# Attention scores on the tensor engine: one product of 32 rows by 128 columns, or four of 32 rows by 32 columns

## The chip, the cores and the metric

The kernel runs on one core of one Trainium2 chip. The metric is the time of one execution on the device in microseconds (us); smaller is better. The kernel before takes 1616.93 us (median of two runs, 1616.18 and 1617.67). The profile was taken in one more execution, whose span from the first to the last instruction is 1615.1 us.

The core has a tensor engine (PE; its weight loads are listed apart as PEld), a vector engine (DVE), a scalar engine (ACT), a general engine (POOL) and queues that start transfers (SP).

## The reference

Two layers, each an attention with 32 heads of 16 elements that share one key and one value head, followed by a mixer and an MLP. Only the attention is touched. Cut to what matters (sequence 2048, width 512):

```python
def _A_ref(x, wq, wk, wv, wo):
    B, S, D = x.shape
    H = 32
    Dh = D // H                                   # 16
    q = (x @ wq).reshape(B, S, H, Dh) ...         # transposed to B, H, S, Dh
    k = x @ wk                                    # S x 16, one for all heads
    v = x @ wv
    scores = jnp.einsum("bhqd,bkd->bhqk", q, k) * (Dh ** -0.5)
    p = _softmax(scores, axis=-1)
    o = jnp.einsum("bhqk,bkd->bhqd", p, v)
    return ... o ... @ wo

x = A_x
x = x + _A_ref(_layernorm(x), A_wq, A_wk, A_wv, A_wo)
x = x + _B_ref(_layernorm(x), ...)                # mixer and MLP
x = x + _A_ref(_layernorm(x), A_wq, A_wk, A_wv, A_wo)
x = x + _B_ref(_layernorm(x), ...)
```

A score product has only 16 elements to sum over. The kernel pads them to 32, so four heads fit side by side into the 128 rows of the tensor engine.

## The kernel before

The program declares operations with their inputs, outputs and an assumed duration. A planner in the same file puts them in order when the program is built, and each engine then runs a fixed list in a fixed order with semaphore waits. Nothing is reordered at run time except what the hardware itself does.

The keys lie four times over in `KT` (rows 0-31, 32-63, 64-95, 96-127), the queries of four heads lie in the same four row groups of `QT`. One call of `qk` makes the scores of one head `h` for 128 keys (or twice 128 keys, where a chunk has only 256 queries) in one bank of `PB`, which is PSUM:

```python
def qk(self, e, g, h, bank):
    la, c, b, kb, nk = g[0:5]
    n = self.size(la, c)                 # 512 queries, or 256 (then nk = 2)
    for j in range(nk):
        ins = e.matmul(self.PB[:, bank, j * n:(j + 1) * n],
                       lhsT=self.KT[32 * h:32 * h + 32, la, (kb + j) * 128:(kb + j + 1) * 128],
                       rhs=self.QT[32 * h:32 * h + 32, self.par(la, c), b, 0:n],
                       start=True, stop=True, tile_position=(32 * h, 0))
    return ins
```

Scores leave PSUM in one of two ways. A *unit* is two heads, made together in one of two pairs of banks and turned into exponentials by one instruction of ACT. A *pair* is two heads whose exponentials are made from integer arithmetic by DVE and POOL; each head of it takes a bank of a small pool.

```python
def declare_unit(self, g):
    b0 = self.ACT_SLOTS[k % 2]                         # banks 0,1 or 2,3
    hs = (2 * g[5], 2 * g[5] + 1)
    def fpe(e):
        for j, h in enumerate(hs):
            ins = self.qk(e, g, h, b0 + j)
        return ins
    q = op("PE", fpe, ..., pe=("Q", 512, 256, hs), prio=0)
    o = q.feeds = op("ACT", lambda e: e.activation(self.EA[:, ea, :, :], self.PB[:, b0:b0 + 2, :],
                                                   ACTF.Exp, scale=0.25), ...)
    ...
def declare_pair(self, g):
    for i in range(2):
        op("PE", lambda e, h=h, L=L: self.qk(e, g, h, L.bank), ..., pe=("Q", 512, 128, (h,)))
        o = op("DVE", lambda e, ...: e.tensor_scalar(out=J[...], in0=self.PB[:, L.bank, :], ...))
    ... # two more scaled copies JK, on POOL or DVE
```

The exponentials go back into the tensor engine against the values (`VP`, `VD`), four products at a time, each with 128 rows and 32 columns, into four partition ranges of the bank `ACC`. All products of the projections, the mixer and the MLP are cut in the same way, by `dot`. Products of zeros by ones (`NIL`, `ONES`), called fillers, are put where the plan would otherwise leave the tensor engine idle, because its clock depends on how busy it is.

```python
def dot(self, e, bank, n, lhsT, rhs, start, stop):
    for g in range(4):
        ins = e.matmul(self.PB[32 * g:32 * g + 32, bank, 0:n], lhsT=lhsT[:, 32 * g:32 * g + 32], rhs=rhs,
                       start=start, stop=stop, tile_position=(0, 32 * g), skip_group_check=True)
    return ins

def declare_pv(self, seg, g, ap, tags, part):
    def fpe(e):
        for j in range(nk):
            for x in range(4):
                i, u = divmod(x, 2)
                ins = e.matmul(self.PB[32 * x:32 * x + 32, self.ACC, p * hw:p * hw + hw], lhsT=v[:, la, kb + j, :],
                               rhs=ap[:, i, j * w + u * hw:j * w + u * hw + hw], start=first and j == 0,
                               stop=False, skip_group_check=True, tile_position=(0, 32 * x))
        return ins
```

The planner knows two kinds of packed products, `"Q"` (the scores) and `"P"` (everything cut in four columns), and reckons 0.097 us for each change between them:

```python
SWITCH = 0.097
def begin(self, o, t):
    if o.pe[0] != self.pe_kind:
        return max(t, self.pe_end + self.SWITCH)
    ...
```

Of the kernel before, what the change touches and what calls it, by code (L numbers as in the profile page):

```python
# [495 lines left out]
class Kernel:  # L496
# [448 lines left out]
    def qk(self, e, g, h, bank):  # L945
        la, c, b, kb, nk = g[0:5]
        n = self.size(la, c)
        ins = None
        for j in range(nk):
            ins = e.matmul(self.PB[:, bank, j * n:(j + 1) * n],  # L950
                           lhsT=self.KT[32 * h:32 * h + 32, la, (kb + j) * 128:(kb + j + 1) * 128],
                           rhs=self.QT[32 * h:32 * h + 32, self.par(la, c), b, 0:n],
                           start=True, stop=True, tile_position=(32 * h, 0))
        return ins

    def filler(self):
# [518 lines left out]
```

The softmax here doesn't subtract the row's maximum and nothing guards it: scores larger than these inputs give would overflow.

## Time and profile before

The profile has 28,953 products and as many weight loads on PE.

| engine | busy us | share of the span | instructions |
|---|---|---|---|
| PE | 1567.6 | 97% | 28953 |
| PEld | 654.9 | 41% | 28953 |
| ACT | 1500.5 | 93% | 1580 |
| DVE | 1245.5 | 77% | 2222 |
| POOL | 1118.4 | 69% | 1083 |

Busy time is the union of the recorded intervals. The recorded interval of a product is longer than the time for which it keeps the next one waiting, because products are pipelined and their ends are modelled; so 97% on PE does not say that PE has no pauses. The starts of the products are the sounder record. The granted clock of PE is 0.999 of full speed over the span. Transfers play no part: 13 GB/s on average.

In the tables of groups, a row gives the source line, the engine, the operation, what is written and read, the tile of the array (rows*columns), the moving operand's shape, the count, then busy time and the mean duration of one, then the idle time of the engine before it and what ended it.

### The profile page before, as it was taken

The page shows a single profiled execution, that of the slowest core. Times are in us where ns is not written, and L with a number is a line of the kernel's source. Part 1 is how long each engine was busy: PE and PEld are TensorE (multiplying, and loading weights), DVE is VectorE, ACT ScalarE, POOL GpSimd, SP SyncE. Part 2 cuts the span into 40 slices and gives each one's busy share as a digit, 9 for nine tenths or more (in the row PEclk, how much of TensorE's full clock was granted, in tenths as well). Part 3 has the DMA queues.
Part 4 walks back from the last instruction along what each step waited for, and adds up shares of the span by engine and source line. Part 5 has one row for each costly group of instructions (what it writes and reads, how often), then busy time and mean ns, then how long its engine had stood idle before and what let it go on. Part 6 is the DMA issues. An engine that isn't in the chain of part 4 may idle for free.

```text
span 1615.1 us, 63788 instructions
## 1 busy us (share of the span) xinstructions
PE 1567.6 (97%) x28953; PEld 654.9 (41%) x28953; DVE 1245.5 (77%) x2222; ACT 1500.5 (93%) x1580; POOL 1118.4 (69%) x1083
## 2 busy tenths in 40 slices
PE   8999999999999999999999999999999999999999
PEld 3333333434333333333333434333343334544555
DVE  8777887778887679887776678878678885778863
ACT  4999999999999999999998499999999998999952
POOL 4798877866787766776673477677777867768631
PEclk9999999999999999999999999999999999999999
DMA  6100010001000001000000000100000000000000
GB/s 207 17 6 5 7 18 6 6 4 17 7 6 4 6 4 19 6 4 2 2 2 2 3 9 9 19 4 5 9 18 5 6 5 15 16 8 7 6 17 19
DMA packets 32144, 21.55 MB, mean 13 GB/s; under 512 B 12672, under 2 KB 31360, under 8 KB 31872
## 3 DMA queue, kind: packets, MB, share of 16 engines
q1 hardware_dynamic: 31872, 17.47, 4.5%
q8 instruction: 226, 3.70, 1.0%
q14 instruction: 46, 0.38, 0.1%
HBM read 7.90 MB, written 2.10 MB: 6 GB/s over the span
## 4 chain that ended last, share of the span: by engine, by line
ACT 64%; PE 33%; DVE 2%; issue 0%; DMA 0%; POOL 0%; SPq 0%; POOLq 0%
ACT EA L994 59%; PE PB L612 12%; PE PB L950 10%; PE PB L1073 8%; ACT G L1403 2%; PE PB L769 1%; ACT L994 1%; ACT GP L1323 1%; ACT L1403 1%; ACT L1323 0%; DVE ZR L752 0%; DVE ST L723 0%; DMA X<-in_A_x_dram 0%; DVE J L1015 0%; PE PB L878 0%
## 5 line engine op out<-in xcount | busy, mean ns | idle before, releaser
L994 ACT ACTIVATE EA<-PB 128x1024 bf16<-128x1024 f32 x1504 | 1390.6, 1105 | 66.6 <-PE PB L1073 33.8
L1025 POOL TENSOR_SCALAR JK<-J 128x1024 uint16<-128x1024 uint16 x983 | 1035.6, 1054 | 402.4 <-DVE J L1015 257.4
L1015 DVE TENSOR_SCALAR J<-PB 128x512 uint16<-128x512 f32 x1088 | 702.4, 683 | 185.1 <-PE PB L950 181.1
L950 PE MATMUL PB<-QT,KT 32*128 32x512 bf16 (+1 forms) x4608 | 624.4, 359 | 30.5 <-ACT EA L994 18.6
L1073 PE MATMUL PB<-EA,VP 128*32 128x256 bf16 (+1 forms) x6784 | 388.4, 265 | 0.5
L950 PEld LDWEIGHTS PB<-QT,KT 32*128 32x128 bf16 x4608 | 161.3, 91 | 448.0 <-ACT EA L994 351.4
L1073 PE MATMUL PB<-JK,VD 128*32 128x256 bf16 (+1 forms) x4864 | 291.3, 265 | 2.9 <-POOL JK L1025 1.9
L1073 PEld LDWEIGHTS PB<-EA,VP 128*32 128x32 bf16 x6784 | 157.1, 95 | 175.3 <-issue 149.6
L612 PE MATMUL PB<-ONES,NIL 128*32 128x512 bf16 x1984 | 177.1, 387 | 7.4 <-DVE ZR L752 2.8
L1073 PEld LDWEIGHTS PB<-JK,VD 128*32 128x32 bf16 x4864 | 114.9, 95 | 128.0 <-issue 78.8
L612 PE MATMUL PB<-ZT,W 128*32 128x512 bf16 (+2 forms) x2816 | 166.6, 341 | 0.0
L1073 PE MATMUL PB<-J,VD 128*32 128x256 bf16 (+1 forms) x2432 | 154.9, 264 | 1.3 <-DVE J L1015 0.8
L612 PE MATMUL PB<-W,G 128*32 128x512 bf16 x1792 | 122.9, 380 | 0.3 <-DVE X L1279 0.3
L1396 DVE CAST G<-PB 128x512 bf16<-128x512 f32 (+2 forms) x126 | 72.3, 582 | 34.7 <-PE PB L612 33.4
L612 PEld LDWEIGHTS PB<-ZT,W 128*32 128x32 bf16 x2816 | 67.7, 96 | 26.1 <-issue 13.0
L1025 DVE TENSOR_SCALAR JK<-J 128x1024 uint16<-128x1024 uint16 x105 | 73.2, 702 | 2.9 <-PE PB L1073 1.9
L1073 PEld LDWEIGHTS PB<-J,VD 128*32 128x32 bf16 x2432 | 60.6, 95 | 35.4 <-issue 21.6
L612 PEld LDWEIGHTS PB<-ONES,NIL 128*32 128x32 bf16 x1984 | 49.6, 96 | 42.4 <-issue 11.2
L745 POOL TENSOR_TENSOR SM<-SM,MH 128x4 f32<-128x4 f32 (+4 forms) x30 | 31.7, 1058 | 40.8 <-DVE SM L737 24.8
L1133 DVE TENSOR_TENSOR OS<-ACCF,PB 128x512 bf16<-128x512 bf16 (+1 forms) x72 | 44.6, 622 | 17.7 <-PE PB L1127 17.3
L612 PEld LDWEIGHTS PB<-W,G 128*32 128x32 bf16 x1792 | 42.2, 96 | 31.8 <-issue 11.7
L1403 ACT ACTIVATE G<-G 128x3584 bf16<-128x3584 bf16 (+2 forms) x18 | 46.0, 2601 | 9.4 <-DVE G L1396 9.3
(88 smaller groups left out, 861.5 us busy)
## 6 DMA issues: line engine op xcount, KB each, us to landing
OT<-OS SPq DMA_DIRECT2D x424, 8.0 KB, 1.8
W<-in_B_w_dram SPq DMA_DIRECT2D x2, 1792.0 KB, 14.4
QT<-QS SPq DMA_DIRECT2D x40, 64.0 KB, 2.4
X<-in_A_x_dram SPq DMA_DIRECT2D x8, 256.0 KB, 5.4
out_dram<-OUTB SPq DMA_DIRECT2D x16, 128.0 KB, 1.7
OT<-OS SPq DMA_DIRECT2D x104, 4.0 KB, 1.7
W<-in_B_w_dram SPq DMA_DIRECT2D x2, 512.0 KB, 8.4
WQ<-in_A_wq_dram SPq DMA_DIRECT2D x1, 512.0 KB, 5.0
```

The source lines that it names most:

```text
L612: ins = e.matmul(self.PB[32 * g:32 * g + 32, bank, 0:n], lhsT=lhsT[:, 32 * g:32 * g + 32], rhs=rhs, start=start, stop=stop, tile_position= ...
L745: op("POOL", lambda e: e.tensor_tensor(out=self.SM[:, 0:k, a:b], in0=self.SM[:, 2:2 + k, a:b], in1=self.MH[:, 0:k, a:b], op=ALU.pow), read ...
L769: ins = e.transpose(self.PBH[:, L.bank, j * 512 + i * 128:j * 512 + (i + 1) * 128], self.ZR[:, tb % 4, dc * 128:(dc + 1) * 128], self.IDENT)
L950: ins = e.matmul(self.PB[:, bank, j * n:(j + 1) * n], lhsT=self.KT[32 * h:32 * h + 32, la, (kb + j) * 128:(kb + j + 1) * 128], rhs=self.QT ...
L994: o = q.feeds = op("ACT", lambda e: e.activation(self.EA[:, ea, :, :], self.PB[:, b0:b0 + 2, :], ACTF.Exp, scale=0.25), writes=bk + [("EA" ...
L1015: o = op("DVE", lambda e, i=i, L=L: e.tensor_scalar(out=J[:, i * 512:(i + 1) * 512], in0=self.PB[:, L.bank, :], scalar1=128 * LOG2E * 0.25 ...
L1025: x = op(eng, lambda e, k=k, r=r: e.tensor_scalar(out=self.JK[:, r, :], in0=J, scalar1=float(self.STEPS[k]), scalar2=1.0, op0=ALU.add, op1 ...
L1073: ins = e.matmul(self.PB[32 * x:32 * x + 32, self.ACC, p * hw:p * hw + hw], lhsT=v[:, la, kb + j, :], rhs=ap[:, i, j * w + u * hw:j * w + ...
L1133: op("DVE", lambda e: e.tensor_tensor(out=self.OS[:, m, 0:n], in0=acc, in1=self.PB[:, M.bank, 0:n], op=ALU.mult), reads=[("ACCF", m)], wri ...
L1323: return e.activation(self.GP[:, par, :, 2:2 + n], self.GP[:, par, :, 2:2 + n], ACTF.Gelu_apprx_tanh)
L1396: op("DVE", lambda e, f=f, L=L: e.tensor_copy(self.G2[:, f, 0:n], self.PB[:, L.bank, 0:n]), writes=[L, ("G2", f)], dur=t_ps(n), give=L)
L1403: ins = e.activation(self.G2[:, a:a + 7, 0:n], self.G2[:, a:a + 7, 0:n], ACTF.Gelu_apprx_tanh)
```

## The change

Each score product with a stationary operand of 32 rows by 128 columns becomes four products with 32 rows by 32 columns. The four take consecutive quarters of the same 128 keys as stationary operand, read the same queries as moving operand, and write the four partition ranges of the same bank. The results and their places are unchanged. The form of the score products comes nearer to that of all the others, whose columns are already cut in four. The order of the operations is not touched, because the costs that the planner assumes are not touched.

```diff
@@ -947,10 +947,12 @@
         n = self.size(la, c)
         ins = None
         for j in range(nk):
-            ins = e.matmul(self.PB[:, bank, j * n:(j + 1) * n],
-                           lhsT=self.KT[32 * h:32 * h + 32, la, (kb + j) * 128:(kb + j + 1) * 128],
-                           rhs=self.QT[32 * h:32 * h + 32, self.par(la, c), b, 0:n],
-                           start=True, stop=True, tile_position=(32 * h, 0))
+            for x in range(4):
+                k0 = (kb + j) * 128 + 32 * x
+                ins = e.matmul(self.PB[32 * x:32 * x + 32, bank, j * n:(j + 1) * n],
+                               lhsT=self.KT[32 * h:32 * h + 32, la, k0:k0 + 32],
+                               rhs=self.QT[32 * h:32 * h + 32, self.par(la, c), b, 0:n],
+                               start=True, stop=True, tile_position=(32 * h, 32 * x), skip_group_check=True)
         return ins
```

## The prediction

> **What bounds the kernel now.** I read the chain of work that ended last first, then the groups, then single products on PE. The chain and the rows of the groups that matter:
>
> ```profile
> ACT 64%; PE 33%; DVE 2%; issue 0%; DMA 0%; POOL 0%; SPq 0%; POOLq 0%
> ACT EA L994 59%; PE PB L612 12%; PE PB L950 10%; PE PB L1073 8%; ACT G L1403 2%; PE PB L769 1%; ACT L994 1%; ACT GP L1323 1%; ACT L1403 1%; ACT L1323 0%; DVE ZR L752 0%; DVE ST L723 0%; DMA X<-in_A_x_dram 0%; DVE J L1015 0%; PE PB L878 0%
> ...
> L994 ACT ACTIVATE EA<-PB 128x1024 bf16<-128x1024 f32 x1504 | 1390.6, 1105 | 66.6 <-PE PB L1073 33.8
> ...
> L950 PE MATMUL PB<-QT,KT 32*128 32x512 bf16 (+1 forms) x4608 | 624.4, 359 | 30.5 <-ACT EA L994 18.6
> ```
>
> The exponentials of ACT (L994) carry 59% of the chain, and PE 33%, of which the score products (L950), the only line that changes, 10%. ACT waits for PE in all only 66.6 us before its exponentials. The table of stretches shows where: ACT is full in most of the attention, and not full where the projections of a chunk come on top (columns: length, then PE, PEld, DVE, ACT, POOL busy with counts, clock of PE, share and rate of transfers).
>
> ```profile
> 300.00:400.00 100.00, 98.67 (x1746) 40.36 (x1744) 75.43 (x132) 99.69 (x104) 69.77 (x67) 1.00 0.03 6
> ...
> 800.00:900.00 100.00, 96.06 (x1666) 40.93 (x1658) 72.44 (x135) 81.82 (x83) 54.29 (x53) 1.00 0.01 2
> 900.00:1000.00 100.00, 96.87 (x1724) 39.58 (x1720) 72.22 (x131) 87.37 (x93) 66.54 (x64) 1.00 0.04 8
> ...
> 1300.00:1400.00 100.00, 97.97 (x2134) 43.46 (x2136) 70.19 (x122) 92.68 (x95) 67.16 (x65) 1.00 0.05 13
> ```
>
> How full PE really is has to be read from the starts of its products. The timeline of PE (start, length, then the group):
>
> ```profile
> 429.87 0.39 PE L950 MATMUL PB<-QT,KT 32*128 32x512 bf16 x2
> 430.19 0.29 PE L1073 MATMUL PB<-EA,VP 128*32 128x256 bf16 x4
> 430.31 0.28 PE L1073 MATMUL PB<-JK,VD 128*32 128x256 bf16 x4
> 430.52 0.65 PE L950 MATMUL PB<-QT,KT 32*128 32x512 bf16 x4
> 431.10 0.29 PE L1073 MATMUL PB<-EA,VP 128*32 128x256 bf16 x4
> 431.22 0.60 PE L612 MATMUL PB<-ONES,NIL 128*32 128x512 bf16 x8
> 431.76 0.39 PE L950 MATMUL PB<-QT,KT 32*128 32x512 bf16 x2
> ```
>
> Two score products start together at 429.87 and the next kind starts 0.32 us later: 512 columns at 2.4 per ns are 0.213, so 0.1 is the change of kind. From 430.31 to 430.52 it is 0.21 for 256 columns (0.107): 0.1 again on the way back. The four products of one value group (x4) start 3.4 ns apart in the single records. I went through all starts: after subtracting the streams (1218 us, with the 3.4 ns steps inside the groups), and 3226 changes of kind at 0.098 us (316 us), only 95 us of pauses are left on PE in the whole span, 56 of them before score products. (The three sums exceed the span by 14 us, because inside one kind the steps of a group hide behind the stream of the group before; ahead of a change of kind they don't.) So PE is nearly as full as ACT. Another sign: a unit's score products may start 56 ns after the exponential that frees their banks (5th percentile), but the median starts after 228 ns, and between 300 and 400 us after 353 ns. Exponentials end 917 ns apart (median), and PE is close behind them.
>
> **What the Trainium skill says.** "TensorEngine Tiling (Array Packing)", section Key Properties, says that a change of tiling mode drains the engine, while different tiles of one mode run in parallel. The trace agrees: 94 to 101 ns at each change, whatever the two shapes (32*128 to 128*32 101, 128*128 to 128*32 96, 32*128 to 128*128 103), and about nothing inside a kind. "TensorE: Matmul & The Clock Gate", section Measured speedup vs the span model, gives about 4 ns per further tile in a pack, up to sixteen tiles of 32 by 32. The trace shows 3.4 ns for four column tiles, and for up to four row tiles too: the time from the first score product of a run to the next kind is 314, 318, 321 and 325 ns for runs of 1, 2, 3 and 4 products of 512 columns (medians of 6, 815, 129 and 365 runs). No run here has sixteen. The same page, section Weight-path perf modes, says that a fast weight load needs all 128 columns, so the change gives it up. In the trace this looks harmless: recorded loads are 91 ns for 128 columns and 92 to 96 for 32, and the first group after a change of kind is longer by 10 to 11 ns in both forms (278 against 267 ns for scores of 256 columns, 283 against 272 for values).
>
> **The change part by part.** It removes 4608 products and loads and puts 18,432 in their place, 13,824 more of each. The streams do not grow: the four quarters run side by side. Waits, semaphores, banks and order stay. What is added is the step inside the group: 13,824 x 3.43 ns (the mean of 20,378 such steps) = 47.4 us of PE. Checked by runs: there are 1528 runs of score products between other kinds, so 31 ns each: 6 more steps (21 ns) in 815 runs of two, 12 more (42 ns) in 365 of four. I expect the change of kind to cost the same: the row size still changes from 32 to 128, and a change of the rows alone (32*128 to 128*128) cost 103 ns. So nothing is gained there.
>
> How much of the 47 us reaches the end? By the chain: L950 holds 9.9% of the span (160 us); at about 0.32 us per run that is 500 runs, times 31 ns = 15.5 us. By stretches: the added time per 100 us is the count of score products x 3 x 3.43 ns, for 300 to 400 us 274 x 10.3 = 2.8 us, against 2.7 us of pauses left on PE there. From 100 us on the pauses per 100 us are 10.7, 6.0, 2.7, 5.9, 3.5, 4.8, 3.5, 7.1, 8.1, 5.8, 4.4, 6.1, 3.6, 4.3; the added time is 2.0 to 3.3, with 3.8 at 1300 and 5.6 at 1400, where a run has twice as many products. If half of the pauses can take it up, and none of those between 800 and 1000, where PE is already on the chain, about 16 us are left over; if a third can, about 24. I take 20: 1617 + 20 = 1637.
>
> **The rivals.** First, the change is free: ACT sets the pace, PE catches up in its pauses, and the time stays within a few us of 1617. For it: ACT waits only 0.7 us for PE between 100 and 700 us. Against it: the late starts (353 ns of some 420 that a unit can be late before ACT idles: 917 less 56 less the 384 to 388 of the products less a second 56). Second, the change of kind gets cheaper, since both kinds now have 32 columns. That would be worth 0.1 us at most of 3226 changes, and ACT would then cap the gain: its 66.6 us of waiting and the 33% of PE in the chain allow perhaps 50 us, to 1570. Against it: 32*128 to 128*128 drains as long as any other change. Third, the loads of 32 columns in one row group don't overlap, and each further quarter costs some tens of ns in place of 3.4; at 25 ns it would be 13,824 x 25 = 346 us, past 1900. Against it: the value groups load four column tiles of the same rows 3.4 ns apart. Fourth, PE's sequencer becomes the bound: between 1400 and 1500 us it would have to issue 2695 + 3 x 548 = 4339 products, one per 23 ns. For it: no stretch shows that rate for long; the fastest 128 products in a row took 2.90 us (22.6 ns each), the fastest 256 took 27.8 ns each. Against it: "TensorEngine Tiling", section Instruction Overhead, gives some 60 cycles per product, but 32 products of 128 columns start here 13.9 ns apart, and no change of kind in the dense part is late without a semaphore (88 to 89 ns in 117 cases). It would add 10 to 30 us in the last 250 us, to about 1660. The clock is a last doubt: if quarter tiles counted less as activity it would fall; the tile area in use is the same, so I give it little.
>
> **Range and chances.** The sum is 0 to 47 us if the step of 3.4 ns holds. Ends of 1619 (nearly all hidden) and 1662 (all exposed, or part of it and some of the fourth rival) should hold it 8 times in 10. Slower by over 2% means above 1649, 32 of the 47 us exposed, or rival three or four: 0.28. Faster by over 2% needs the second rival: 0.03. Within 2%: 0.69.
>
> **What would show it.** Right: 42,777 products on PE; steps of 3.4 ns inside score groups of 8; 338 ns from the first score product of a unit to the next kind, and 366 ns for four heads; about 0.1 us at each change; pauses before score products down from 56 us to some 30; late starts of units up; idle time of ACT before L994 up from 66.6 to 80 to 90 us, most of it where PE is on the chain; clock at 1.00. Wrong: steps well above 3.4 ns or loads that end the wait (third rival), changes of kind under 80 ns (second), stretches at 1370 to 1550 us that lose far more than 5 us per 100 us (fourth), or a clock below 0.95.

## The result, and the profile after

The changed kernel takes 1692.44 us (median of two runs, 1689.84 and 1695.05) against 1616.93: 75.5 us more, a ratio of 1.0465 with a 95% interval of 1.0445 to 1.0485. The prediction was 1637 with a range of 1619 to 1662.

The page of the kernel after first: the clock by slices, the chain that ended last by engine and by line, and the rows of the exponentials (now L996) and of the score products (now L952).

```profile
PEclk9999999999999999999999999999999998997999
...
PE 53%; ACT 41%; DVE 3%; issue 2%; POOL 1%; DMA 0%; SPq 0%; POOLq 0%
ACT EA L996 38%; PE PB L952 19%; PE PB L612 16%; PE PB L1075 15%; PE PB L769 2%; ACT G L1405 1%; DVE J L1017 1%; ACT L996 1%; PE PB L1129 1%; ACT GP L1325 0%; ACT L1405 0%; POOL JK L1027 0%; PE PB L1114 0%; DVE ZR L752 0%; PE PB L811 0%
...
L996 ACT ACTIVATE EA<-PB 128x1024 bf16<-128x1024 f32 x1504 | 1416.7, 1062 | 113.4 <-PE PB L952 73.0
...
L952 PE MATMUL PB<-QT,KT 32*32 32x512 bf16 (+1 forms) x18432 | 677.3, 364 | 34.0 <-ACT EA L996 13.9
```

PE has taken over the chain (53% for 33%), ACT waits 113.4 us before exponentials (66.6 before), and late in the run there are slices in which the clock was granted only in part. Before, there were none.

Where the time went shows when the same exponential is looked up in both traces: there are 1504, in the same order, counted from 0 here. The table gives how much later each one ends in the changed kernel (worked out from the single records):

| exponential | ends, before | later by |
|---|---|---|
| 250th | 254.7 us | 0.9 us |
| 500th | 502.3 us | 5.4 us |
| 800th | 804.9 us | 10.4 us |
| 1300th | 1337.6 us | 19.2 us |
| 1350th | 1399.3 us | 28.8 us |
| 1400th | 1450.2 us | 40.3 us |
| 1450th | 1496.2 us | 56.0 us |
| 1503rd | 1549.3 us | 72.9 us |

Up to the 1300th the loss is a slow drift, 19 us in 1300. In the last 200 exponentials it is 54 us. These belong to the last two chunks of the second layer, which have 256 queries in place of 512, so that every product of the attention has half the columns and there are twice as many. Two stretches of 20 us from there (columns: length, then PE, PEld, DVE, ACT and POOL busy with counts, clock, share and rate of transfers), before and then after:

```profile
1440.00:1460.00 20.00, 19.77 (x526) 9.38 (x518) 15.79 (x29) 19.94 (x20) 14.81 (x16) 1.00 0.03 7
```

```profile
1440.00:1460.00 20.00, 17.64 (x700) 8.75 (x697) 12.82 (x25) 17.39 (x19) 10.31 (x10) 1.00 0.05 9
```

The changed kernel has 700 products in 20 us, 28.6 ns each, while PE is *less* busy than before (17.64 for 19.77) and so is every other engine. Its timeline on PE shows what the missing time looks like (start, length, group, then idle time and what ended it):

```profile
1434.92 0.29 PE L1075 MATMUL PB<-JK,VD 128*32 128x128 bf16 x8
1435.04 0.28 PE L1075 MATMUL PB<-EA,VP 128*32 128x128 bf16 x8
1435.15 0.28 PE L1075 MATMUL PB<-J,VD 128*32 128x128 bf16 x8
1435.37 0.45 PE L952 MATMUL PB<-QT,KT 32*32 32x256 bf16 x26
1436.98 0.39 PE L952 MATMUL PB<-QT,KT 32*32 32x256 bf16 x6 [1.16 <-issue]
```

One run of 32 score products breaks after the 26th. The next starts after 1.16 us of idle time, and it waits for no semaphore: "issue" means that nothing in the profile holds it. Such breaks come at 1422.2, 1425.5, 1429.1, 1432.7, 1435.6 and 1439.9 us, every 3.6 us or so, in the middle of whatever PE is doing, value products and fillers as well. At the same rate a queue that brings the program's instructions starts a packet of 16 KB: at 1423.6, 1427.2, 1430.9, 1434.6, 1438.2 us. An instruction has 64 bytes (the page counts 91,436 instructions for 5.85 MB on the two instruction queues), so a packet is 256 instructions. This queue serves PE alone: its 334 packets are what 42,777 loads and as many products fill. So a packet is 128 loads and 128 products.

The single records tie the two together. In the chunks of 256 queries (1380 to 1625 us) PE is idle for more than 150 ns without a semaphore 34 times, and each time the next product is the 84th to 86th of 128, counted from the start of the program. Each time PE goes on 1.2 to 1.5 us after a packet has landed, and the next packet starts 1.1 to 1.7 us after that. The packet itself takes 0.9 to 1.4 us. So PE waits for a block to come, and the next one starts only once PE is running again; it is not bandwidth that runs short (all transfers together average 14 GB/s, 13 before). The kernel before has no such pause.

The table of waits between 1380 and 1625 us counts the breaks in its rows on "issue" (total us, times, longest):

```profile
PEld PB L1075 <- issue: 37.9, 145, 1.2
PEld PB L952 <- issue: 35.6, 72, 1.5
...
PE PB L952 <- issue: 12.2, 17, 1.3
```

Before, between 1358 and 1550 us, the score products' loads wait 1.7 us for "issue" in all:

```profile
PEld PB L950 <- issue: 1.7, 5, 0.4
```

(The rows on L1075, the value products, hold the short time at each change of kind too; before, the same products stand at L1073.)

The theory, A: PE's instructions arrive in blocks of 128 loads and products, one block about every 3.7 us (the median from 1380 to 1625 us), and the chunks of 256 queries now ask for more. The first 19 us of the loss are the steps inside the groups. The rivals: B, each added product costs the same everywhere (75.5 us / 13,824 = 5.5 ns); C, the clock alone; D, the form of 32 by 32 itself.

### The profile page after: what moved, and what is told of

Its sections match the earlier page's. It is cut to its first block, busy times and chain, and to the rows that moved or that the text cites. A ratio compares the mean times of both kernels' runs of the same rounds, so it can differ in the third digit from the quotient of the medians.

```text
span 1688.0 us, 91436 instructions
## 1 busy us (share of the span) xinstructions
PE 1627.8 (96%) x42777; PEld 702.6 (42%) x42777; DVE 1247.1 (74%) x2222; ACT 1526.6 (90%) x1580; POOL 1118.9 (66%) x1083
## 4 chain that ended last, share of the span: by engine, by line
PE 53%; ACT 41%; DVE 3%; issue 2%; POOL 1%; DMA 0%; SPq 0%; POOLq 0%
ACT EA L996 38%; PE PB L952 19%; PE PB L612 16%; PE PB L1075 15%; PE PB L769 2%; ACT G L1405 1%; DVE J L1017 1%; ACT L996 1%; PE PB L1129 1%; ACT GP L1325 0%; ACT L1405 0%; POOL JK L1027 0%; PE PB L1114 0%; DVE ZR L752 0%; PE PB L811 0%
## 5 line engine op out<-in xcount | busy, mean ns | idle before, releaser
L996 ACT ACTIVATE EA<-PB 128x1024 bf16<-128x1024 f32 x1504 | 1416.7, 1062 | 113.4 <-PE PB L952 73.0
L952 PE MATMUL PB<-QT,KT 32*32 32x512 bf16 (+1 forms) x18432 | 677.3, 364 | 34.0 <-ACT EA L996 13.9
L1075 PE MATMUL PB<-EA,VP 128*32 128x256 bf16 (+1 forms) x6784 | 393.1, 268 | 2.4 <-issue 1.6
L952 PEld LDWEIGHTS PB<-QT,KT 32*32 32x32 bf16 x18432 | 201.7, 88 | 452.1 <-ACT EA L996 301.6
L1075 PE MATMUL PB<-JK,VD 128*32 128x256 bf16 (+1 forms) x4864 | 294.8, 268 | 3.9 <-POOL JK L1027 1.7
L1075 PEld LDWEIGHTS PB<-EA,VP 128*32 128x32 bf16 x6784 | 159.7, 96 | 181.4 <-issue 156.0
L1075 PEld LDWEIGHTS PB<-JK,VD 128*32 128x32 bf16 x4864 | 116.6, 96 | 130.0 <-issue 82.2
L1075 PE MATMUL PB<-J,VD 128*32 128x256 bf16 (+1 forms) x2432 | 156.7, 266 | 3.0 <-issue 1.2
L1075 PEld LDWEIGHTS PB<-J,VD 128*32 128x32 bf16 x2432 | 61.6, 97 | 37.7 <-issue 24.1
```

Of the source, the lines that this page charges most:

```text
L952: ins = e.matmul(self.PB[32 * x:32 * x + 32, bank, j * n:(j + 1) * n], lhsT=self.KT[32 * h:32 * h + 32, la, k0:k0 + 32], rhs=self.QT[32 * ...
```

## The experiments

### Each part of the change alone

```diff
   # in qk, shortened: one product of 128 columns becomes 128 // w of w columns
+  w = 32 if n == 512 else 128        # wide: quarters only with 512 queries
+  w = 128 if n == 512 else 32        # narrow: quarters only with 256 queries
   for j in range(nk):
+      for x in range(128 // w):
           ins = e.matmul(self.PB[w * x:w * x + w, bank, ...], lhsT=self.KT[..., k0:k0 + w], ...)
```

> Four products of 32 columns only where a chunk has 512 queries (10,752 of the 13,824 added products); the chunks of 256 queries keep 128 columns. Theory A (instructions of PE arrive in blocks of 16 KB, 128 loads and products, about every 3.6 us; the two chunks of 256 queries ask for more than that and wait for blocks; elsewhere only the steps inside the groups cost): 1617 + 20 = 1637 us, no long pauses without a wait in the chunks of 256 queries, clock 1.00. Rival B (every added product costs the same, 75.5 us / 13,824 = 5.5 ns, wherever it is): 1617 + 59 = 1676 us.

Measured: 1636.21 us, ratio 1.0120 (1.0104 to 1.0135).

> The other part alone: four products of 32 columns only where a chunk has 256 queries (3,072 added products). Theory A: the stretch of these chunks is as slow as in the changed kernel, 1617 + 53 = 1670 us, with pauses every 3.6 us and stretches at half clock. Rival B: 1617 + 17 = 1634 us.

Measured: 1667.40 us, ratio 1.0317 (1.0300 to 1.0334). So 78% of the added products cost 19.5 us, and the other 22% cost 50.7. Rival B had it the other way round and is gone. The two sum to 70 of the 75.5 us. The exponentials show that each part acts where it is: with quarters only at 512 queries the 1306th exponential is 18.9 us late and no more than 0.5 is added after it; with quarters only at 256 queries it is 0.8 us late and 50.5 are added after it. There, the breaks are back:

```profile
PEld PB L953 <- issue: 34.5, 59, 1.6
...
PE PB L953 <- issue: 14.8, 18, 1.3
```

### PE with nothing but products

This kernel leaves out the whole computation and writes zeros. PE runs products of 128 rows by 32 columns in four column tiles without any wait for another engine.

```diff
+for n, k in ((512, 1536), (320, 2048), (256, 2048), (128, 2048), (64, 2048)):
+    for i in range(k):
+        g = i % 4
+        e.matmul(PB[32 * g:32 * g + 32, i // 4 % 8, 0:n], lhsT=W[:, 32 * g:32 * g + 32], rhs=R[:, 0:n],
+                 start=True, stop=True, tile_position=(0, 32 * g), skip_group_check=True)
```

> Leaves out the whole computation: PE alone runs products of 128 rows by 32 columns in four column tiles, without waits, first 1536 with 512 columns moving, then 2048 each with 320, 256, 128 and 64; the output is zeros. Theory A: 54 and 34 ns per product at 512 and 320, where the array is the bound; then it stops falling: about 27 to 29 ns at 256, 128 and 64 alike, in bursts with a pause every 128 products. Without a limit of supply it is 54, 34, 27, 14 and 7 ns.

Measured, from the first to the last start of each part: 55.6, 33.9, 28.7, 29.5 and 28.4 ns per product. It stops falling at 28 to 29 ns, although in proportion to the first part the array would need only 14 and 7 ns at 128 and 64 columns. The timeline of the part with 128 columns:

```profile
221.69 1.97 PE L27 MATMUL PB<-R,W 128*32 128x128 bf16 x128 [1.49 <-issue]
225.41 1.97 PE L27 MATMUL PB<-R,W 128*32 128x128 bf16 x128 [1.76 <-issue]
229.42 1.97 PE L27 MATMUL PB<-R,W 128*32 128x128 bf16 x128 [2.03 <-issue]
```

After the first 95 products of this part a pause, mostly of 1.3 to 2 us, follows each 128th exactly, and the instruction queue starts packets of 16 KB 3.3 to 4.3 us apart (most at 3.4 to 4.0). Again PE goes on 1.2 to 1.6 us after a packet has landed. In the part with 512 columns the packets are 6.9 us apart, as fast as they are used up. Between the pauses products start 14 ns apart, so it is not the issue of one instruction that is slow: the next block isn't there. No other engine and no other transfer is at work here, so nothing of the attention kernel is needed for the limit.

The clock falls in this kernel too. The table of stretches gives it for the parts with 128 and with 64 columns (columns: length, then PE, PEld, DVE and POOL busy with counts, clock, share and rate of transfers):

```profile
220.00:270.00 50.00, 28.29 (x1680) 26.21 (x1669) 0.00 (x0) 0.00 (x0) 0.93 0.02 4
280.00:330.00 50.00, 24.85 (x1680) 22.97 (x1683) 0.00 (x0) 0.00 (x0) 0.50 0.02 4
```

At half the clock the products come no more slowly (28.4 ns) than at a clock of 0.93 (29.5 ns), so the pace of the blocks does not follow the clock of PE.

### The same number of instructions without touching the scores

If it is the number alone, any other products will do.

```diff
 # value products, only where a chunk has 256 queries: 128 moving columns become two times 64
+q = 64 if hw == 128 else hw
 for j in range(nk):
+  for a in range(0, hw, q):
     for x in range(4):
-        e.matmul(... self.ACC, p*hw : p*hw + hw ...)
+        e.matmul(... self.ACC, p*hw + a : p*hw + a + q ...)
```

> The score products stay at 32 rows by 128 columns everywhere. In the chunks of 256 queries each value product of 128 moving columns is cut into two of 64: 3,072 more products and loads, the same number that the quarters added there, with the same streams and in the form of all the other products. Theory A (supply of instructions, 28.1 ns per load and product): as slow as quarters in these chunks, 1617 + 45 to 51 = 1662 to 1668 us, pauses without waits every 3.6 us. Rival D (the form of 32 by 32, or the steps ahead of a change of kind, is what costs): 1617 to 1622 us.

Measured: 1672.45 us, ratio 1.0345 (1.0328 to 1.0362), 4 us above the range of theory A. All of it is lost in the chunks of 256 queries (0.2 us up to the 1306th exponential, 55.5 after it), at pauses of the same kind: 29 times PE is idle for more than 150 ns without a semaphore, each at the end of a block. The score products are as in the kernel before, 32 by 128, so rival D is out: neither their form nor the steps ahead of a change of kind make the 51 us.

### How the loss grows with the number added

Two products of 64 columns everywhere add 1,024 in the chunks of 256 queries and 3,584 in the others:

```diff
+  w = 64
```

> Two products of 64 columns everywhere (4,608 added products). Theory A: the stretch with 256 queries then asks for one load and product per 30.7 ns, slower than blocks come (27.7 ns), so nothing waits for blocks and a third of the steps remains: 1617 + 9 = 1626 us, clock 1.00. Rival B: 1617 + 25 = 1642 us. If a little waiting for blocks is left at the densest places, 1628 to 1632.

Measured: 1636.01 us, ratio 1.0119 (1.0104 to 1.0134): twice what theory A gave. In the dense stretch it is right: 3.5 us are lost after the 1306th exponential, the clock is at 0.999, no break without a wait is over 150 ns. The miss is in the chunks of 512 queries, 14.1 us up to the 1306th. The timeline shows why:

```profile
451.22 0.41 PE L953 MATMUL PB<-QT,KT 32*64 32x512 bf16 x4
451.56 0.29 PE L1076 MATMUL PB<-J,VD 128*32 128x256 bf16 x4
```

From the first of the four products to the next kind it takes 338 ns (median of 815 runs). Four products of 128 columns take 325, eight of 32 columns 338. Four of 64 columns should be like the former, and are 13 ns longer; each is recorded with 398 ns, not 384. The recorded loads are longer as well, 101 ns for 91. This fits "TensorE: Matmul & The Clock Gate" of the Trainium skill, section Weight-path perf modes: a load is fast only with all 128 columns, and its time goes with the columns. By that reading, 32 columns without the fast load take about as long as 128 with it (88 and 91 ns recorded), and 64 take longer; no run here switched the fast load alone. So halves save two thirds of the steps and pay a longer load at each change of kind.

Between halves and the full cut, the value products were cut in two sorts out of three, and in one:

```diff
-q = 64 if hw == 128 else hw
+q = 64 if hw == 128 and part is None else hw      # only those on VP: 1,536 more
+q = 64 if hw == 128 and part != 0 else hw         # those on VP and JK: 2,560 more
```

> As the cut of the value products in the chunks of 256 queries, but only those on ACT's exponentials (VP): 1,536 more products and loads. The stretch from the 1306th exponential to the last takes 204 us and holds 5,392 products; with these 6,928, which at 28.5 ns are 197 us. Theory A (supply, a threshold): 1617 + 3 to 10 us, short pauses only at the densest places. A cost in proportion to the number added (55.4 us for 3,072): 1617 + 28 = 1645 us.

Measured: 1630.50 us, ratio 1.0092 (1.0064 to 1.0120): 13 us more, above the 3 to 10 of theory A and less than half of the 28 of proportion.

> The same with the products on ACT's exponentials and on the copies JK: 2,560 more products. 7,952 at 28.5 ns are 227 us, 22 more than 204; with stretches at half clock 5 to 8 more. Theory A: 1617 + 22 to 32 us. In proportion: 1617 + 46 = 1663 us.

Measured: 1662.82 us, ratio 1.0283 (1.0262 to 1.0305): the number of theory A was too low here, and the line of proportion happens to pass there. Over the whole range the line doesn't hold: the loss after the 1306th exponential is 3.5, 13.1, 42.3 and 55.5 us for 1,024 (halves of scores), 1,536, 2,560 and 3,072 (values) added products, 3.4 ns each for the first thousand, 19 for the next 512, then 29 and 26 ns. That is a bend between 1,000 and 1,500 (the first point cuts scores, the others values), and after it the price of a place in a block. My two numbers failed because I compared averages: with 2,560 more the stretch ran at 29.9 ns per product at full clock, not 28.5 (7,834 products x 1.4 = 11 us), and 20.5 us of it were at half clock. An uneven demand would do this, since a block that isn't fetched while PE waits for something else can't come faster later; no run tests this by itself.

### Taking PE time away elsewhere

```diff
-lambda e: self.dot(e, bank, 512, self.NIL, self.ONES, ...)
+lambda e: self.dot(e, bank, 256, self.NIL, self.ONES[:, 0:256], ...)
```

> The kernel before with fillers of 256 in place of 512 columns (496 fillers, 53 us of PE less; nothing else leaves). If PE is nearly as full as ACT, as the late starts of score products say, a good part comes back: 1617 - 15 to 30 = 1587 to 1602 us, as long as the clock holds. If ACT alone sets the pace: 1617. If the clock falls to half for long: above 1640.

Measured: 1622.15 us, ratio 1.0027 (1.0016 to 1.0038), slightly slower. The expectation fell.

> Four products of 32 columns where a chunk has 512 queries, and the short fillers of 256 columns. If the 19.5 us of that part are PE time added on a PE that is nearly full, PE time taken elsewhere gives about as much back: 1636 - 15 to 30 = 1606 to 1621 us at full clock. If they come from something else than PE time, it stays at 1636.

Measured: 1637.76 us, ratio 1.0128 (1.0113 to 1.0143); again nothing came back. With short fillers on the kernel before, the exponentials end at the same time as before to 0.2 us up to the 600th; 3.4 us are lost about the 640th and 3.0 about the 865th, each at a stretch of half clock that the profile of the kernel before doesn't have (10.2 us from 634 us on, 6.8 from 884). The fillers lie where PE would pause anyway, so their 53 us were worth nothing as time, and kept the clock up. That PE is nearly full on average says nothing of what a microsecond is worth at a given place. It doesn't contradict that the added steps cost something: by hundreds of us, quarters at 512 queries lose 0.2 us where PE had 10.7 us of pauses (100 to 200), and 2.1 of 2.8 where it had 2.7 (300 to 400).

## Why the prediction was wrong

**The steps inside the groups: right.** The steps are 3.3 ns, the time from the first score product of a unit to the next kind is 338 ns and for four heads 365 (predicted 338 and 366).

```profile
451.10 0.43 PE L952 MATMUL PB<-QT,KT 32*32 32x512 bf16 x16
451.46 0.40 PE L1075 MATMUL PB<-JK,VD 128*32 128x256 bf16 x8
451.69 0.39 PE L1075 MATMUL PB<-EA,VP 128*32 128x256 bf16 x8
452.01 0.41 PE L952 MATMUL PB<-QT,KT 32*32 32x512 bf16 x8
452.35 0.29 PE L1075 MATMUL PB<-J,VD 128*32 128x256 bf16 x4
```

The sixteenth score product starts 50 ns after the first, and the value products follow 0.36 us after the first; for eight, 0.34.

**What of them reaches the end: right.** 19.5 us measured where a chunk has 512 queries, alone; 10,752 x 3.43 = 37 us are added there, so about half is hidden, as the sum over stretches had it. Counted in that kernel as the prediction counts them, the pauses before score products fall from 56 to 41 us: they take up 15 us. One sign of it was misjudged. ACT's idle time before exponentials is 70.5 us there, not 80 to 90; the recorded exponentials overlap, and they overlap less (1105 ns each before, 1069 there), so the loss hardly shows as idle time.

**The change of kind: right.** It still costs 91 to 104 ns in the medians; 32*32 to 128*32 saves nothing, and the second rival is out. The third is out too: nothing serialises in the loads.

**The supply of instructions: this is the step that failed.** The fourth rival was named with the right place and the right demand, one product per 23 ns between 1400 and 1500 us, and was sized at 10 to 30 us and then left out of the sum. With quarters only there, 50.7 us were lost. Two things were mis-sized. First, the limit: I took the fastest 128 products in a row (22.6 ns each) as a rate that can be had, where 128 is no more than one block already fetched. The fastest 256, 27.8 ns each, lie near the limit that the runs then showed; but nothing in the kernel before waited for blocks, so that profile alone could not show it as one. At the 28.4 to 29.5 ns of the kernel with nothing but products, the 8,402 products of the stretch after the 1306th exponential need 239 to 248 us. The stretch took 197 us before and 251 after, so the supply by itself accounts for 42 to 51 of the 54 us lost there (an estimate from these figures). Second, "no change of kind is late without a semaphore" was true and proved nothing: a limit of supply doesn't show below itself.

The page "Runtime: NRT & Kernel Launch" of the Trainium skill, section Instruction fetch mechanics, has the mechanism: each engine's instructions are refilled in blocks of 16 KiB, 256 instructions, and the cost of a block is "mostly hidden". The blocks are as it says; hidden they are not, here, once 128 loads and products take PE under 3.6 us.

**The clock: a part of it.** I gave it little. In the last two chunks the changed kernel has 44 us at half clock, with 1,122 products at 39.5 ns each, against 28.3 in the rest of that stretch: 1,122 x 11.2 = 13 us of the 54, by this estimate, which overlaps with the one for the supply. With quarters at 256 queries alone it is 27 us and 670 products, 8 us; the difference is as large as the 5 us by which the two parts fall short of the whole, but no run shows that it is the same 5 us. The breaks seem to let PE's activity fall and so the clock: in the kernel with nothing but products, too, the clock falls only after the pauses have begun. No run here changed the clock with the supply kept, so this is not shown. Rival C, the clock as the whole cause, is out: between 1440 and 1500 us the clock is 1.00, and the exponentials lose 11 us there.

## What to carry to other kernels

Cutting a product into smaller tiles keeps the streams and multiplies instructions: count loads and products per us in the densest stretch, not over the span, and compare it with what PE can be fed for more than two blocks in a row (here 28 to 29 ns per load and product). A rate seen over 128 products is a buffer, not a supply. A pause that no semaphore ends, that comes back after the same number of instructions on whatever line, and that ends a fixed time after a packet of the instruction queue has landed, points to a fetch.

## What the hardware showed that I had not expected

- Where PE waits for its instructions, it gets a block of 128 loads and products about every 3.7 us in the kernel (median) and 3.4 to 4.0 us with nothing else running. There, that is 28.4 to 29.5 ns for each pair, at 128 or 64 columns and at full or half clock.
- The transfer is the smaller part of that time: 0.9 to 1.4 us of it. In the kernel PE goes on 1.2 to 1.5 us after the landing, and the next packet starts 1.1 to 1.7 us later.
- A score tile of 64 columns costs 13 ns more at a change of kind than one of 128 or of 32 columns (338 against 325 ns for four products of 64 and of 128). A unit takes 338 ns in halves as in quarters, and 318 whole.
- Fillers cut by half take 53 us off PE, some 22 of them in the first 600 us, where no exponential moved by over 0.2 us; later the clock fell twice, and 5 us were lost in all.
